# Attention and a squared-ReLU MLP in one hand-ordered kernel: another order for the first head pair and the weights, and other chunks transposed by TensorE

## The chip, the cores and the metric

The kernel runs on one core of a Trainium2 chip. The metric is device time in microseconds (us) of one execution; lower is better. The kernel before took 880.01, 882.34 and 882.65 us in three runs, a median of 882.34 us. One more execution was profiled: it took 878.6 us, and its span from the first to the last instruction is 876.7 us. All rows come from that execution.

## The reference

```python
# q, k, v: (4, 8, 1152, 64) float32; w_in: (512, 2048); w_out: (2048, 512)
q_pool = q.reshape(B, H, S // 2, 2, D).mean(axis=3)             # 576 queries a head
scores = (1 / sqrt(D)) * matmul(q_pool, k.transpose(0, 1, 3, 2))
scores = scores - max(scores, axis=-1, keepdims=True)
attn = exp(scores)
attn = attn / (sum(attn, axis=-1, keepdims=True) + 1e-09)
x = matmul(attn, v)                    # then (batch, query) rows, heads side by side: (2304, 512)
h = x @ w_in
out = maximum(h, 0) ** 2 @ w_out       # (2304, 512)
```

All products are made of two float16 halves of each float32 operand (a high part and what is left of it, after a scaling by powers of two), in three products each.

## The kernel before

**The work.** Four batches of eight heads are taken as 16 head pairs. Each pair is prepared once (`prep`, L346): its k, q and v are loaded (`LK`, `LQ`, `LV` on SP's queue, L365 and L373), neighbouring queries are summed (`QS`, L384), scales are found, the float16 halves are made (`KA`/`KD`, `QA`/`QD`, `VA`/`VD`, L315 to L343), and k and q are transposed by the DMA engines (`KT` L488, `QT` L503) and copied to a second place (`QX`, L509). Then the pair's queries go through in nine chunks of 128 (`chunk`, L540), 144 chunks in all: scores on TensorE (`S`, six matmuls of 128 rows; in one chunk of nine both heads share the rows and there are twelve), row maximum on VectorE (`MX`, L580), exponential on ScalarE (`EX`, L591). The probabilities must then be transposed, and there are two ways:

- By the DMA engines: high half (`HI`, on ScalarE, GpSimd or VectorE), low half (`LO`, L603, on VectorE or GpSimd), one DMA transpose (`TR`, L615).
- By TensorE, for the chunks listed in `TURNB`: three times three transposing matmuls against the identity into a PSUM bank (`TP`, L658), the high half by ScalarE (`TH`, L667), the low half by VectorE (`TL`, L681).

Every ninth chunk (numbers 6, 15, 24 ...) is the shared one and is always transposed by DMA, even where `TURNB` lists it. Per pair, two groups of 54 matmuls multiply the transposed probabilities by v (`PV`, L723).

**The weights.** `weights` (L946) takes each matrix in eight halves of 1 MB: load (`WL`, L967, SP's queue), two ScalarE passes (`W1`, `W2`), and three VectorE passes `W3` (L982), `W5` (L986) and `W4` (L995; `W4` may go to GpSimd instead). There are two staging buffers, so the load of half c waits for the passes of half c - 2. Then TensorE and VectorE find a scale (`WG`, `WM`, `WS1` to `WS3`), and each quarter is split (`WA` on ScalarE, `WD` on VectorE, L343).

**The MLP.** There are nine blocks of 256 tokens (`block`, L746). A block may start when the four pairs of its batch have passed the chunks that it needs (block 0 after chunk 30, block 1 after chunk 35, blocks 2 and 3 after chunks 66 and 71, and so on; the last three after chunks 138 to 143) and when the weights are split. It normalises and splits its x (`RV` to `XD`), then runs eight times 24 matmuls with w_in (`H`, L865), each followed by `HA`, `G1`, `G2`, `G3` on ScalarE, VectorE and GpSimd, and eight times 12 matmuls with w_out (`O`, L914).

**The order.** Every engine runs its instructions in a fixed order, which a planner (`Plan`, L57) writes before the kernel is built. Each step has a list of engines that it may run on with an assumed cost, the steps that it depends on, and a priority:

```python
prio = cfg("nudge", {}).get(len(self.ops), 0.0) + at + off.get(kind, DEF.get(kind, 0.0)) \
       + (off0.get(kind, 0.0) if at < self.early else 0.0)
```

A lower number goes first. `at` is the number of the chunk that the step belongs to; for a pair's preparation it is `need`, the number of the pair's first chunk; for half c of the weights it is `c * WSP + WOF`. `off` is a number per kind of step, `off0` a second one that is added for steps with `at` below 31, `nudge` a number per single step. On each engine the planner looks at the steps that could start within a slack (`slPE`, `slACT`, ...) of the earliest one and takes the one with the lowest priority. SP issues all DMAs, in the planned order: an issue whose wait is not yet fulfilled holds those behind it.

Of the kernel before, what the change touches and what calls it, by code (L numbers as in the profile page):

```python
# [20 lines left out]
def cfg(k, d):  # L21
    return CFG.get(k, d)

# [187 lines left out]
def kernel(  # L211
# [13 lines left out]
    B, H, S, D = q.shape  # L225
# [7 lines left out]
    KD = DM // 128  # L233
# [76 lines left out]
    def raw(*key):  # L310
        return raws[plan.slot[key][1]]
# [21 lines left out]
    def scale_b(t):  # L333
# [3 lines left out]
        )  # L337

    def pmul(out, x, s0, s1=1.0):
        nc.gpsimd.tensor_scalar(out, x, s0, s1, op0=ALU.mult, op1=ALU.mult)  # L340

    def split_lo(o, x, s, h):
        nc.vector.scalar_tensor_tensor(out=o, in0=x, scalar=s, in1=h, op0=ALU.mult, op1=ALU.subtract)  # L343


    def prep(n):  # L346
        pair = preps[n]["pair"]
        b, hp = divmod(pair, NP)
        need = preps[n]["need"]
        slot = preps[n]["slot"]  # L350
        p0 = preps[n]["old"]
        old = [("S", preps[p0]["last"])] if p0 is not None else []
        oldv = [("PV", *preps[p0]["lastg"])] if p0 is not None else []

        def rk():
            return raw("k", n).rearrange("p (h c d) -> p h c d", h=2, c=9)

        def rv():
            return raw("v", n).rearrange("p (h c d) -> p h c d", h=2, c=9)

        def rq():
            return raw("q", n).rearrange("p (c r d) -> p c r d", c=9, r=2)
# [724 lines left out]
    preps, visits, chunks, groups, pairs_, gidx, eds, exs = [], [], [], [], [], {}, {}, {}  # L1087
# [52 lines left out]
    for n in range(len(preps)):  # L1140
        prep(n)
# [52 lines left out]
```

## Time and profile before

| what | value |
|---|---|
| runs shown | 880.01, 882.34, 882.65 us (median 882.34) |
| profiled execution | 878.6 us, span 876.7 us |
| TensorE busy (PE) | 85% of the span |
| VectorE busy (DVE) | 661.3 us, 75% |
| ScalarE busy (ACT) | 601.0 us, 69% |
| GpSimd busy (POOL) | 380.5 us, 43% |
| mean granted TensorE clock | 0.966 of full speed |
| main DMA queue | 130.05 MB, 74.0% of 16 engines over the span |

How to read it: the shares are means over a kernel with three stages, a first one until the MLP's first block, a middle one until the last chunk, and a tail with the MLP alone. Which engine limits differs between them, so the rows further down are taken stage by stage. Busy time of an engine that is not the limit costs nothing.

### The profile page before, as it was taken

What the parts mean: (1) busy time and instruction counts of PE and PEld (TensorE: products, weight loads), DVE (VectorE), ACT (ScalarE), POOL (GpSimd) and SP (SyncE); (2) the same over time, 40 slices, a digit from 0 to 9 for tenths busy, and PEclk for the clock granted to TensorE, in tenths of its full rate; (3) what the DMA queues carried; (4) which work ended last, traced back from release to release, by engine and by line L of the source; (5) the groups of instructions that cost most, each with busy time, mean ns of one, the idle gap of its engine ahead of it and who ended that gap; (6) DMA issues with size and microseconds to landing.
All of it is one profiled execution on the core that took longest, in us unless ns stands there. A gap on an engine that the chain in (4) does not pass through costs nothing. (4 is left out here: it accounts for less than half of the span.)

```text
span 876.7 us, 15564 instructions
## 1 busy us (share of the span) xinstructions
PE 745.9 (85%) x6077; PEld 501.0 (57%) x6077; DVE 661.3 (75%) x838; ACT 601.0 (69%) x957; POOL 380.5 (43%) x274
## 2 busy tenths in 40 slices
PE   1367766577679998999799999999999899999997
PEld 0234454444457565754576667558665666857673
DVE  5788999999998788878988788897889783422120
ACT  5468669668877779787789768679868873524250
POOL 1155542335368445656686337634854740000000
PEclk9999987899879999999999999999999999999999
DMA  7986776885587989989999998899999975000001
GB/s 256 302 208 99 144 195 173 167 184 100 111 174 138 199 166 211 165 176 166 203 181 178 171 181 171 177 172 180 173 190 192 157 136 94 13 13 13 13 13 25
DMA packets 337545, 131.04 MB, mean 149 GB/s; under 512 B 320832, under 2 KB 320832, under 8 KB 337472
## 3 DMA queue, kind: packets, MB, share of 16 engines
q1 hardware_dynamic: 337472, 130.05, 74.0%
q8 instruction: 48, 0.79, 0.4%
q14 instruction: 25, 0.20, 0.1%
HBM read 45.09 MB, written 4.72 MB: 57 GB/s over the span
## 5 line engine op out<-in xcount | busy, mean ns | idle before, releaser
L580 DVE TENSOR_REDUCE ca<-s 128x1 f32<-128x1152 f32 x144 | 192.6, 1348 | 11.9 <-PE s L572 8.6
L603 POOL TENSOR_TENSOR buf<-buf,buf 128x1152 f16<-128x1152 f32 x65 | 163.8, 2522 | 86.2 <-ACT buf L595 67.7
L591 ACT ACTIVATE buf<-s,ca,esc 128x1152 f32<-128x1152 f32 x144 | 188.8, 1311 | 8.4 <-DMA PT<-buf 0.9
L865 PEld LDWEIGHTS <-w 128*128 128x128 f16 x1728 | 168.7, 99 | 29.5 <-issue 3.6
L572 PE MATMUL s<-kT,qT 128*128 128x512 f16 (+1 forms) x768 | 152.4, 340 | 35.9 <-ACT buf L591 24.4
L914 PE MATMUL ba<-w,region 128*128 128x512 f16 x624 | 142.8, 379 | 0.9 <-DVE region L797 0.4
L914 PEld LDWEIGHTS <-region 128*128 128x128 f16 x864 | 83.2, 98 | 94.1 <-issue 2.1
L865 PE MATMUL ba<-region,w 128*128 128x256 f16 x1104 | 126.4, 273 | 2.0 <-DVE PT L681 1.3
L572 PEld LDWEIGHTS <-qT 128*128 128x128 f16 x768 | 69.0, 102 | 102.5 <-issue 41.0
L723 PE MATMUL ba<-PT,v 128*64 128x256 f16 (+1 forms) x1728 | 119.5, 297 | 6.2 <-DVE PT L681 5.5
L723 PEld LDWEIGHTS <-v 128*64 128x64 f16 x1728 | 102.8, 114 | 22.3 <-issue 14.0
L590 ACT ACTIVATE ca<-ca,cols,esc 128x1 f32<-128x1 f32 x144 | 54.8, 381 | 58.1 <-DVE ca L580 57.6
L603 DVE TENSOR_TENSOR buf<-buf,buf 128x1152 f16<-128x1152 f32 x47 | 79.6, 1694 | 19.7 <-ACT buf L595 13.4
L892 DVE TENSOR_TENSOR region<-region 128x512 f16<-128x512 f32 x39 | 39.3, 1009 | 69.3 <-ACT region L885 69.2
L340 POOL TENSOR_SCALAR buf<-buf,cols 128x1152 f16<-128x1152 f32 x30 | 40.4, 1348 | 74.1 <-ACT buf L591 51.8
L658 PE MATMUL ba<-ident,buf 128*128 128x128 f32 x288 | 52.3, 303 | 21.6 <-DVE PT L681 16.6
L595 ACT ACTIVATE buf<-buf 128x1152 f16<-128x1152 f32 x58 | 67.4, 1162 | 3.2 <-DMA PT<-buf 1.1
L667 ACT ACTIVATE PT<-ba 128x384 f16<-128x384 f32 x96 | 44.5, 483 | 32.6 <-PE ba L658 27.8
L892 POOL TENSOR_TENSOR region<-region 128x512 f16<-128x512 f32 x33 | 48.1, 1460 | 31.8 <-ACT region L885 24.5
L658 PEld LDWEIGHTS ba<-ident,buf 128*128 128x128 f32 x288 | 33.9, 152 | 40.4 <-DVE PT L681 25.2
L343 DVE SCALAR_TENSOR_TENSOR buf<-raw,psc,buf 128x576 f16<-128x576 f32 x48 | 53.3, 1147 | 4.6 <-POOL buf L317 3.8
L681 DVE TENSOR_TENSOR PT<-ba,PT 128x384 f16<-128x384 f32 x96 | 50.7, 549 | 4.8 <-ACT PT L667 4.4
(133 smaller groups left out, 949.5 us busy)
## 6 DMA issues: line engine op xcount, KB each, us to landing
raw<-in_k_dram SPq DMA_DIRECT2D x16, 576.0 KB, 4.8
raw<-in_q_dram SPq DMA_DIRECT2D x32, 288.0 KB, 4.4
raw<-in_v_dram SPq DMA_DIRECT2D x16, 576.0 KB, 4.4
region<-in_moe_w_in_dram SPq DMA_DIRECT2D x8, 1024.0 KB, 6.1
region<-in_moe_w_out_dram SPq DMA_DIRECT2D x8, 1024.0 KB, 6.1
out_dram<-buf SPq DMA_DIRECT2D x36, 128.0 KB, 2.4
PT<-buf SPq DMA_TRANSPOSE x128, 4.8
qT<-buf SPq DMA_TRANSPOSE x32, 4.2
```

Of the source, the lines that this page charges most:

```text
L343: nc.vector.scalar_tensor_tensor(out=o, in0=x, scalar=s, in1=h, op0=ALU.mult, op1=ALU.subtract)
L572: nc.tensor.matmul(s[:, x, :w], lhsT=qt[:, l, h, c0 : c0 + 2, :].rearrange("p a b -> p (a b)"), rhs=rhs, **st)
L580: nc.vector.reduce_max(a[:, 0:1], st3(), axis=AX.X)
L590: nc.scalar.activation(a[:, 1:2], a[:, 0:1], AF.Identity, bias=ln14, scale=tl["esc", n][:, 0:1])
L591: nc.scalar.activation(P(), st3(), AF.Exp, bias=a[:, 1:2], scale=tl["esc", n][:, 2:3], accum_out=col)
L595: nc.scalar.activation(hl()[:, 0], P(), AF.Copy)
L603: e.tensor_tensor(out=hl()[:, 1], in0=P(), in1=hl()[:, 0], op=ALU.subtract)
L658: nc.tensor.matmul(t[:, y], lhsT=P()[:, c * 128 : (c + 1) * 128], rhs=ident, is_transpose=True, start=(y == 0), stop=False, skip_group_che ...
L723: nc.tensor.matmul(px[h * 64 : (h + 1) * 64, :N], lhsT=vv[:, h, kc, vl, :], rhs=t[:, 9 * pl + kc, :N], start=(i == 0), stop=(i == 3 * NC - ...
L865: nc.tensor.matmul(ph[:, f2], lhsT=w16[0][:, SLOT[f // 4], wl, a, f % 4 * 128 : (f % 4 + 1) * 128], rhs=xhl()[:, xl, a], start=(i == 0), s ...
L892: e.tensor_tensor(out=gt[u][:, 1], in0=rt[u % 2], in1=gt[u][:, 0], op=ALU.subtract)
L914: nc.tensor.matmul(p[:, :DM], lhsT=g[:, gl, f % 2, tt * 128 : (tt + 1) * 128], rhs=w16[1][:, SLOT[f // 4], wl, f % 4], start=(f == 0 and g ...
```

## The change

The code changes in one line of `prep`, and the table of constants `CFG` is replaced as a whole. The diff, with the long line broken up and cut to what is used below:

```diff
-CFG = {'SPLIT': 0, 'TURN': [],
-  'TURNB': [0, 1, 3, 4, 6, 7, 9, 10, 12, 13, 15, 16, 18, 19, 21, 22, 24, 25, 27, 28, 30, 31, 33, 34,
-            40, 49, 58, 67, 76, 85, 94, 103, 112, 121, 130, 139],
-  'WSP': 0.1, 'WOF': 21.58, 'MSP': 113.61, 'pen': 1179.24, 'bl': 2.88,
-  'slPE': 18.29, 'slACT': 71.85, 'slDVE': 10.76, 'slPOOL': 168.16, 'slSP': 469.69,
...
-  'nudge': {0: 4.83, 1: -37.14, 2: 6.88,
...
+CFG = {'SPLIT': 0, 'TURN': [],
+  'TURNB': [0, 2, 4, 6, 8, 10, 12, 14, 16, 18, 20, 22, 24, 26, 28, 30, 32, 34,
+            38, 44, 50, 56, 62, 68, 74, 80, 86, 92, 98, 104, 110, 116, 122, 128, 134],
+  'WSP': 1.668, 'WOF': 0.15, 'MSP': 16.28, 'pen': 805.54, 'bl': 2.27,
+  'slPE': 253.17, 'slACT': 48.62, 'slDVE': 147.59, 'slPOOL': 732.63, 'slSP': 123.78,
...
@@ prep
-        need = preps[n]["need"]
+        need = preps[n]["need"] if n else cfg("P0", -1000)
```

- `P0` is not set, so every step of the first pair's preparation gets 1000 taken off its priority number.
- `TURNB`: leaving out the shared chunks, TensorE turns 20 of the first 36 chunks before and 16 after, and 12 of the later 108 before and 17 after; in all 32 before and 33 after.
- The 1662 single `nudge` numbers are gone, and nearly all numbers of `off` and `off0` are others.

Sums of `off` and `off0` for steps with `at` below 31, to which `at` is still added:

| step | before | after |
|---|---|---|
| `WL` (weight load) | -156 | 640 |
| `LK`, `LQ`, `LV` (loads of a pair) | 702, -456, 32 | -77, -318, -927 |
| `KT`, `QT` (transposes of a pair) | 123, 814 | -70, -133 |
| `TR` (transpose of a chunk by DMA) | 2583 | 80 |
| `W3`, `W5`, `W4` | 935, 2196, 62 | 0, 0, 480 |
| `MX`, `TL` | 341, -2344 | 0, 0 |
| `WS1`, `WD` | 3414, 257 | -287, -100 |
| `S` | 2168 | 723 |

For later steps `off` alone counts: `S` 2350 before and 728 after, `H` 3380 and 998, `O` 3483 and 1003, `RV` 382 and 968, `XD` 520 and 875, `MX` 735 and 0. The weights' `at` is 21.6 to 23.1 before and 0.15 to 25.2 after.

## Rows read from the trace of the kernel before

**Rows 1.** The page, busy time and share of the span: TensorE.

```profile
PE 745.9 (85%) x6077; PEld 501.0 (57%) x6077; DVE 661.3 (75%) x838; ACT 601.0 (69%) x957; POOL 380.5 (43%) x274
```

**Rows 2.** Busy time by stretch: start:end, length, engines, granted clock, DMA share, GB/s.

```profile
core 0: us, PE busy (x) PEld busy (x) DVE busy (x) ACT busy (x) POOL busy (x), PEclk, DMA share, GB/s
0.00:249.00 249.00, 147.92 (x1208) 101.24 (x1208) 221.72 (x312) 173.99 (x266) 95.29 (x72) 0.90 0.75 178
...
300.00:400.00 100.00, 92.15 (x785) 60.44 (x784) 83.02 (x104) 78.18 (x127) 52.49 (x35) 1.00 0.93 177
...
600.00:700.00 100.00, 96.45 (x811) 67.44 (x810) 84.02 (x95) 81.66 (x132) 62.55 (x44) 1.00 1.01 181
...
745.00:877.00 132.00, 126.65 (x901) 83.86 (x898) 30.48 (x50) 45.47 (x71) 2.59 (x7) 0.99 0.06 15
...
249.00:720.00 471.00, 446.32 (x3750) 300.32 (x3749) 400.01 (x461) 372.60 (x607) 278.15 (x191) 0.99 0.94 175
```

**Rows 3.** Two lines' instructions: duration min/median/max in ns, first and last start in us.

```profile
L865 PE MATMUL ba<-buf,w x192: 270/273/418, 249.4 to 282.9; 128*128 128x256 f16 x192
...
L572 PE MATMUL s<-kT,qT x768: 217/379/635, 43.4 to 719.6; 128*128 128x512 f16 x128, 128*128 128x128 f16 x64
```

**Rows 4.** Two stretches within the first stage, columns as in Rows 2.

```profile
0.00:50.00 50.00, 10.87 (x75) 8.25 (x75) 33.32 (x54) 24.82 (x26) 9.37 (x16) 1.00 0.85 264
60.00:98.00 38.00, 28.45 (x229) 17.57 (x229) 34.46 (x47) 30.55 (x58) 21.23 (x15) 0.96 0.56 94
```

**Rows 5.** Groups of instructions from 60 to 98 us: busy us, mean ns.

```profile
L580 DVE TENSOR_REDUCE ca<-s 128x1 f32<-128x1152 f32 x12 | 16.2, 1348 | 2.1 <-PE s L567 2.1
```

**Rows 6.** Timeline of the start: start us, duration us, engine, line, idle before.

```profile
6.04 1.12 ACT L973 ACTIVATE w<-region 128x1024 f32<-128x1024 f32 x1 [4.03 <-DMA region<-in_moe_w_in_dram]
...
11.38 1.16 ACT L424 ACTIVATE buf<-raw 128x1152 bf16<-128x1152 f32 x1 [0.60 <-DMA raw<-in_k_dram]
...
21.05 3.67 SPq L488 DMA_TRANSPOSE kT<-buf  x1
...
37.08 2.62 SPq L503 DMA_TRANSPOSE qT<-buf  x2
```

**Rows 7.** Groups of instructions from 0 to 249 us: busy us, mean ns.

```profile
L580 DVE TENSOR_REDUCE ca<-s 128x1 f32<-128x1152 f32 x41 | 55.2, 1348 | 4.6 <-PE s L572 2.5 <-PE s L567 2.1
L681 DVE TENSOR_TENSOR PT<-ba,PT 128x384 f16<-128x384 f32 x63 | 32.8, 549 | 1.9 <-ACT PT L667 1.7
...
L343 DVE SCALAR_TENSOR_TENSOR w<-w,wS 128x2048 f16<-128x2048 f32 x6 | 14.9, 2482 | 0.9 <-ACT w L315 0.8
L986 DVE SCALAR_TENSOR_TENSOR w<-region,w 128x1024 int32<-128x1024 int32 x12 | 14.5, 1219 | 0.2
L995 DVE TENSOR_TENSOR w<-w,region 128x1024 f32<-128x1024 f32 x9 | 13.9, 1547 | 0.6
...
L603 DVE TENSOR_TENSOR buf<-buf,buf 128x1152 f16<-128x1152 f32 x7 | 11.2, 1598 | 0.5 <-ACT buf L595 0.4
...
L995 POOL TENSOR_TENSOR w<-w,region 128x1024 f32<-128x1024 f32 x3 | 9.1, 3045 | 15.0 <-DVE w L986 15.0
...
L982 DVE TENSOR_SCALAR w<-w 128x1024 int32<-128x1024 int32 x12 | 8.5, 712 | 5.4 <-ACT w L973 5.4
```

**Rows 8.** The chain that ended last, in order of time: start us, duration us, what.

```profile
586.21 0.48 PE ba L658 x3
...
798.97 10.48 PE bt L865 x96
809.45 10.36 PE bt L914 x48
```

**Rows 9.** One line's instructions on VectorE: duration min/median/max in ns, first and last start.

```profile
L343 DVE SCALAR_TENSOR_TENSOR buf<-raw,psc,buf x48: 798/812/2924, 18.7 to 676.5; 128x576 f16<-128x576 f32 x48
```

**Rows 10.** The page, DMA issues: KB each where given, us to landing.

```profile
PT<-buf SPq DMA_TRANSPOSE x128, 4.8
```

More of the change, by code (lines that the diff above doesn't have):

```diff
@@ new lines @@
+CFG = {'SPLIT': 0, 'TURN': [], 'TURNB': [0, 2, 4, 6, 8, 10, 12, 14, 16, 18, 20, 22, 24, 26, 28, 30, 32, 34, 38, 44, 50, 56, 62, 68, 74, 80, 86, 92, 98, 104, 110, 116, 122, 128, 134], 'WSP': 1.668, 'WOF': 0.15, 'MSP': 16.28, 'pen': 805.54, 'bl': 2.27, 'slPE': 253.17, 'slACT': 48.62, 'slDVE': 147.59, 'slPOOL': 732.63, 'slSP': 123.78, 'off': {'ED': 3.52, 'EX': 0.0, 'G1': 7.57, 'G2': -327.77, 'G3': -712.51, 'GE': 106.11, 'GF': 11.28, 'GM': 7.35, 'GR': -83.1, 'GS': -1554.06, 'GT': -483.92, 'GU': -943.96, 'GW': -608.85, 'H': 998.13, 'HA': 10.05, 'HI': 377.45, 'KA': 232.61, 'KD': 45.75, 'KT': -37.51, 'LK': 178.06, 'LO': 0.72, 'LQ': -446.41, 'LV': -890.99, 'MX': -0.36, 'O': 1002.78, 'OD': -136.82, 'PV': 5.84, 'QA': 1161.12, 'QD': 2.42, 'QK': -788.49, 'QQ': -490.45, 'QS': -624.29, 'QT': -130.75, 'QV': 44.07, 'QX': -736.0, 'RB': 697.5, 'RT': 179.66, 'RU': -42.77, 'RV': 967.54, 'S': 728.2, 'ST': 651.1, 'TH': -2.8, 'TL': -0.45, 'TP': 223.84, 'TR': 26.67, 'VA': 719.74, 'VD': -0.52, 'W1': -5.34, 'W2': 7.86, 'W3': 0.0, 'W4': 36.64, 'W5': 1.5, 'WA': -59.96, 'WD': 181.92, 'WG': 6.6, 'WL': 180.89, 'WM': -115.09, 'WS1': -308.61, 'WS2': -41.81, 'WS3': 18.25, 'XA': 738.07, 'XD': 874.54, 'XM': 838.79, 'XN': 168.03, 'XQ': -6.7, 'XR': -25.78, 'XT': 0.0, 'XU': 94.88, 'XW': 10.01}, 'off0': {'ED': 19.7, 'EX': 1.01, 'G1': 44.88, 'G2': -74.75, 'G3': 109.76, 'GE': -8.18, 'GF': -61.9, 'GM': -3.34, 'GR': -9.85, 'GS': 8.14, 'GT': 63.75, 'GU': 6.06, 'GW': -288.87, 'H': 34.55, 'HA': -8.75, 'KA': 15.81, 'KD': -539.25, 'KT': -32.95, 'LK': -254.97, 'LO': 205.23, 'LQ': 128.8, 'LV': -36.39, 'MX': 0.34, 'O': 22.13, 'OD': 319.51, 'PV': 195.02, 'QA': 22.78, 'QD': 1.87, 'QK': -403.17, 'QQ': 91.93, 'QS': -23.54, 'QT': -2.01, 'QV': 3.19, 'QX': 8.95, 'RB': -51.42, 'RT': 17.45, 'RU': -96.74, 'RV': 17.25, 'S': -5.7, 'ST': 299.89, 'TH': 5.76, 'TP': -260.82, 'TR': 53.57, 'VA': -160.55, 'VD': -209.53, 'W1': 7.54, 'W2': -5.28, 'W3': -0.41, 'W4': 443.7, 'W5': -1.5, 'WA': 37.68, 'WD': -281.84, 'WG': -47.46, 'WL': 458.79, 'WM': -80.6, 'WS1': 21.36, 'WS2': -123.29, 'WS3': -260.63, 'XA': -110.52, 'XD': 12.63, 'XM': 11.88, 'XN': -21.54, 'XQ': -51.95, 'XT': -93.0, 'XU': 70.78, 'XW': -103.32}}
```

1 line of the change is left out of this document (removed).

## The prediction

> **What bounds the kernel now.** I read the totals first, then the stages, then the start, then the pieces on VectorE and the chain. By the totals TensorE is busy for 745.9 us of 876.7 [rows 1], so its idle time is 131 us, and the stages show where it lies [rows 2]. From 0 to 249 us it idles for 101 us while VectorE is busy for 221.7 of 249. From 249 to 720 us it idles for 24.7 us in 471, and in the tail for about 5. The cut at 249 us is no accident: the first `H` matmul starts at 249.4 us, and the last scores at 719.6 us [rows 3]. Until the MLP's first block may start, TensorE has only the chunks, whose pace VectorE sets; from then on it has MLP work to fill every gap. So the kernel is bound by VectorE up to the first `H` and by TensorE after it, and the end moves with two things: when the first `H` starts, and how many chunks are already done by then.
>
> **A formula for the end.** From the first `H` to the end are 627.7 us, of which some 30 are idle (24.7 and 5.3) [rows 2]. A block costs 2 x 10.48 us for `H` (96 of its 192 matmuls take 10.48) and 2 x 10.36 for `O` [rows 8], nine blocks 375 us. The other 222 us belong to the chunks left: 41 row maxima were taken by 249 us [rows 7], so 103 were left, at 2.16 us of TensorE each. Hence
>
> end = T + 375 + 2.16 x (144 - n) + 30,
>
> with T the start of the first `H` and n the chunks done by then: 249 + 375 + 222 + 30 = 876.
>
> T itself: the first scores start at 43.4 us [rows 3]. With almost no weight work, from 60 to 98 us, 12 chunks pass in 38 us [rows 4, 5], 3.17 us each. So 43.4 + 41 x 3.17 = 173.4, and the other 75.6 us up to 249 are weight work after the first scores and losses. A chunk done ahead of the first `H` costs 3.17 us and saves 2.16 later, so each one fewer there gains 1.0 us.
>
> **First pair ahead.** In the kernel before two weight loads stand ahead of the first pair's k, whose first use is at 11.4 us; the pair's own arithmetic is ready for `KT` at 21.1 us, but `QT` is issued at 37.1 us, behind weight loads that wait for their buffers, and the first scores follow 6.3 us later [rows 3, 6]. A first load is used at 6.0 us [rows 6], so k can be taken about 5 us earlier, `QT` be issued at 16 us, and the first scores start at about 22 us (an estimate from these rows). The bounds are 22 and 43: if `QT` still stood behind a weight load, nothing would be won. I take 22, since in the changed list every step of this pair is 1000 ahead of all others on every queue, SP's among them. But this gain is not all kept. VectorE is busy for 33.3 us of the first 50 [rows 4], with weight passes for the most part. By the first scores it had done six halves, 0.71 + 1.22 + 1.22 us each with the short `W4` [rows 7], 19 us. What isn't done then must be done later; while the new order waits for pair 0, it may do two halves (6 us). So 13 us of weight work move behind the first scores, and the start is worth 21 - 13 = 8 us.
>
> **Weights among the chunks.** After the change `W3` and `W5` of half c stand at 1.67c + 0.15 beside `MX` at i, so the weights are spread evenly over chunks 0 to 25 and `WD` follows at once, while block 0 needs chunk 30. Before, 41 chunks were done when the weights were; I take n = 36 (bounds 33, two chunks after chunk 30, and 47, below), a gain of 5 us.
>
> **`W4` to GpSimd.** Its number goes from 62, ahead of `MX`, to 480, behind it, and the planner gives GpSimd a step where VectorE has more urgent work waiting. Before, ten of sixteen ran on VectorE, 13.9 us for nine [rows 7]. The bounds are 0 and 15 us off T; I take 5, since GpSimd takes 3.05 us for one [rows 7] and the choice is unclear. Here a row speaks against the change: the split of k on VectorE takes 812 ns in the median, but up to 2924 [rows 9], so something holds VectorE back by up to 2.1 us at a time, and the nearest suspect is GpSimd at work beside it. The Trainium skill, SBUF — State Buffer, section "SBUF: two separate sides", says that GpSimd and a VectorE instruction with two SBUF inputs share a pair of ports under an exclusive lock, and that whoever comes second is blocked for the whole instruction. By that rule a step moved to GpSimd isn't free, the 5 us would go and the sum would be 5 us higher; the trace agrees in so far as the longest split exceeds the median by not much less than one GpSimd instruction. The median split shows that most steps aren't held, so I keep the 5 us and make the hold a rival.
>
> **Fewer turned early, more later.** Four chunks fewer turned among the first 36 take 4 x 3 x 549 ns = 6.6 us from VectorE [rows 7] and add four `LO`, of which VectorE took a good third (7 of 19 early, 1.6 us each) and some `HI`: net about 3 us off T. TensorE's own part, 4 x 3 x 0.48 us = 5.8 us [rows 8], is hidden, since it idles there. Later it isn't: five chunks more are turned where TensorE is full, 5 x 3 x 0.48 = 7.2 us on the end. Against that stand five DMA transposes fewer, 4.8 us each from issue to landing [rows 10], where the DMA engines are 94% busy [rows 2]; I count that as nothing, since the chain there is TensorE's, not DMA's.
>
> **The other numbers.** The middle stage gets an order without the single-step corrections. Its TensorE idle time lies between 3.5 and 7.9 us in 100 us in the two stretches shown [rows 2], so over 471 us between 17 and 37 us against 24.7 now: -8 to +12. I take +4, since `RV` and `XD` now stand far behind `MX` and a block may be normalised later. In the tail nothing but MLP matmuls is left, and they stay.
>
> **Sum.** 876.7 - 8 (start) - 5 (n) - 5 (`W4`) - 3 (fewer turned) + 7 (more turned) + 4 (middle) = 866.7, or 10 us less. The profiled execution took 878.6 us, so 868.6; the median of the three runs is 882.3, 0.4% above that execution, which would give 872.3. I forecast 869 us.
>
> **Rivals.**
>
> 1. The weights come late, and the kernel is slower. `WL` falls from first (-156) to last (640) on SP's queue, behind every `TR` (80) and every pair load. Place: the loads of halves 4 to 15. While chunks pass at full pace the DMA engines are 56% busy [rows 4], which leaves 44%; a half of 1 MB takes 4 us at the 264 GB/s of the first 50 us [rows 4]; twelve halves need 48 us, which at 44% are 109 us or 34 chunks, nearly the 36 of the forecast. A transpose that waits ahead of a load in the queue tips it over. Price: 1.0 us a chunk beyond 36, so it decides from n = 47 on; at n = 58 the end comes 12 us later than now, 891 us. For it: SP's order and the narrow margin. Against it: chunks slow down while weights are worked on, which leaves the DMA more room.
> 2. Work is moved and not removed: all that VectorE doesn't do at the start it does later, and the `W4` stay where they are. Then the 8 and the 5 us fall away, n and fewer turned chunks (8 us) stand against more turned ones (7 us), and the end is at 869 + 13 = 882 us, the median of now. For it: VectorE is already busy for 89% of the first stage [rows 2].
> 3. GpSimd stands in VectorE's way: seven steps more on GpSimd (five `W4`, two `LO`), each holding VectorE back by the 2.1 us above [rows 9], put 15 us on T in place of 8 off it: 869 + 8 + 15 = 892 us. Against it: GpSimd is busy for only 95 us of 249 [rows 2], and the median split is short. (The rule of the Trainium skill, SBUF — State Buffer, named above, speaks for this rival.)
> 4. More than forecast: all `W4` leave VectorE (10 us more), n is 33 (3 more), and the middle stage reaches its best stretch (12 more): 844 us.
>
> **Numbers.** Forecast 0.50, rival 1 0.20, rival 2 0.14 (mostly no change), rival 3 0.08, rival 4 0.08. A measurement of this kernel tells about 0.3% (2.6 us) from no change. Faster: forecast and rival 4, 0.58; same: 0.11, out of rival 2; slower: rivals 1 and 3 and the rest of 2, 0.31. The forecast's own range, by the bounds of `W4`, n and the middle stage, is 852 to 880. The range reaches to most of rival 1 and half of rival 4: 848 to 891.
>
> **What would show it.** Right: the first scores at about 22 us; the first `H` near T = 249 - 8 - 5 x 3.17 - 5 - 3 = 217 us with about 36 row maxima done; ten or more `W4` on GpSimd; TensorE idle for about 30 us in the middle; the last scores near 710 us (103 chunks in 470 us before, 4.6 us each, now 108 from 217 us on). Wrong: first scores still after 35 us (the pair isn't ahead); a first `H` after 250 us with more than 47 chunks done and weight loads spread beyond 150 us (rival 1); k splits far above 1 us in the mean (rival 3); or TensorE idle for more than 40 us after the first `H`, by which the new list of numbers, not one of its steps, would have decided.

## The result, and the profile after

The changed kernel takes 885.88 us (median of 20 runs, 880.99 to 890.46) against 880.22 us for the kernel before (20 runs, 878.4 to 883.7): a ratio of 1.0058, 95% interval 1.0045 to 1.0072. It is 0.6% slower; the forecast was 869 us, 1.3% below 880.22. The profiled execution took 886.4 us, with a span of 884.2 (before: 878.6 and 876.7).

The page after, busy time of the engines, to be read against [rows 1]:

```profile
PE 753.6 (85%) x6086; PEld 500.6 (57%) x6086; DVE 658.8 (75%) x842; ACT 594.0 (67%) x950; POOL 380.5 (43%) x281
```

Hardly anything moves in the totals, so the stages have to be read. Busy time after, by stretch, cut at the first `H` and at the last scores (columns as in [rows 2]):

```profile
0.00:262.50 262.50, 161.03 (x1272) 104.61 (x1273) 227.73 (x309) 186.65 (x279) 139.99 (x94) 0.82 0.82 187
262.50:730.50 468.00, 443.66 (x3747) 299.10 (x3746) 392.22 (x471) 351.15 (x584) 237.16 (x177) 0.99 0.87 165
730.50:884.20 153.70, 148.85 (x1071) 96.94 (x1069) 38.85 (x66) 56.24 (x89) 3.34 (x10) 1.00 0.14 27
```

The first `H` and the first and last scores after (first and last start at the end of the counts), to be read against [rows 3]:

```profile
L865 PE MATMUL ba<-buf,w x192: 269/273/283, 262.5 to 300.2; 128*128 128x256 f16 x192
...
L572 PE MATMUL s<-kT,qT x768: 217/379/634, 24.9 to 730.5; 128*128 128x512 f16 x128, 128*128 128x128 f16 x64
```

The first scores come at 24.9 us in place of 43.4, nearly as forecast (22). But the first `H` comes at 262.5 us in place of 249.4; forecast was 217. After it TensorE idles for 24.3 us up to the last scores and for 4.9 after them, the 30 us of before. VectorE's groups from 0 to 262.5 us (busy us, mean ns), to be read against [rows 7], and then, of GpSimd's, the one of `LO` and the two of `W4`:

```profile
L580 DVE TENSOR_REDUCE ca<-s 128x1 f32<-128x1152 f32 x47 | 62.8, 1347 | 4.8 <-PE s L572 4.7
L681 DVE TENSOR_TENSOR PT<-ba,PT 128x384 f16<-128x384 f32 x54 | 28.8, 549 | 7.0 <-ACT PT L667 6.9
L343 DVE SCALAR_TENSOR_TENSOR buf<-raw,psc,buf 128x576 f16<-128x576 f32 x18 | 25.1, 1424 | 1.6 <-POOL buf L317 1.4 <-ACT buf L315 0.2
L986 DVE SCALAR_TENSOR_TENSOR w<-region,w 128x1024 int32<-128x1024 int32 x12 | 16.5, 1372 | 0.1
...
L982 DVE TENSOR_SCALAR w<-w 128x1024 int32<-128x1024 int32 x12 | 11.7, 974 | 0.3 <-ACT w L973 0.2
L603 DVE TENSOR_TENSOR buf<-buf,buf 128x1152 f16<-128x1152 f32 x4 | 7.0, 1758 | 0.8 <-ACT buf L595 0.6 <-POOL buf L340 0.2
L995 DVE TENSOR_TENSOR w<-w,region 128x1024 f32<-128x1024 f32 x5 | 7.0, 1390 | 0.2
...
L603 POOL TENSOR_TENSOR buf<-buf,buf 128x1152 f16<-128x1152 f32 x23 | 60.9, 2648 | 24.1 <-DVE buf L599 10.6 <-ACT buf L595 10.4 <-issue 2.3
...
L995 POOL TENSOR_TENSOR w<-w,region 128x1024 f32<-128x1024 f32 x7 | 16.9, 2426 | 20.9 <-DVE w L986 18.6 <-DVE psc L440 2.3
...
L995 POOL TENSOR_TENSOR region<-region 128x1024 f32<-128x1024 f32 x3 | 6.9, 2304 | 0.0
```

The same in the kernel before, from 0 to 249 us, of GpSimd's `LO` and of the split of k and q on VectorE (L343):

```profile
L603 POOL TENSOR_TENSOR buf<-buf,buf 128x1152 f16<-128x1152 f32 x12 | 31.5, 2622 | 17.0 <-ACT buf L595 14.0 <-issue 1.5 <-DVE buf L599 1.0
...
L343 DVE SCALAR_TENSOR_TENSOR buf<-raw,psc,buf 128x576 f16<-128x576 f32 x18 | 16.0, 919 | 3.2 <-POOL buf L317 2.5 <-ACT buf L315 0.6
```

47 row maxima are taken before the first `H`, 41 before [rows 7]. The change did take work off VectorE: `TL` 28.8 us for 32.8, `LO` 7.0 for 11.2, `W4` 7.0 for 13.9 in the group shown. But other instructions got longer with nothing changed about them: the 12 `W3` shown here from 8.5 to 11.7 us, the 12 `W5` from 14.5 to 16.5, and the split of k and q from a mean of 0.92 us to 1.42, with a median of 0.82. (It goes the other way too: VectorE's eight copies `QX` take 3.6 us in place of 9.9.) GpSimd has more to do beside them: in this stage it is busy for 140.0 us in place of 95.3, with 23 `LO` in place of 12 and ten `W4` in place of six. VectorE's busy time in this stage is 6.0 us more than before, and its idle time 34.8 us in place of 27.3; at the start it waits for 9.9 us at one stretch, until the first pair's scales can be found, where its longest wait was 5.4.

**The balance.** T is 13.1 us later. From there on 97 chunks are left in place of 103, 6 x 2.16 = 13.0 us less, against 7.2 us for five more turned ones: 13.1 - 13.0 + 7.2 = 7.3 us, and the span is 7.5 longer. So the prediction's formula holds (262.5 + 375 + 2.16 x 97 + 7 + 29 = 883); what it was fed with, T and n, did not.

### The profile page after: what moved, and what is told of

Same layout as the page of the kernel before. It is cut to its first block, busy times and chain, and to the rows that moved or that the text cites. A ratio compares the mean times of both kernels' runs of the same rounds, so it can differ in the third digit from the quotient of the medians.

```text
span 884.2 us, 15570 instructions
## 1 busy us (share of the span) xinstructions
PE 753.6 (85%) x6086; PEld 500.6 (57%) x6086; DVE 658.8 (75%) x842; ACT 594.0 (67%) x950; POOL 380.5 (43%) x281
## 5 line engine op out<-in xcount | busy, mean ns | idle before, releaser
L572 PE MATMUL s<-kT,qT 128*128 128x512 f16 (+1 forms) x768 | 161.2, 354 | 27.4 <-ACT buf L591 23.6
L603 POOL TENSOR_TENSOR buf<-buf,buf 128x1152 f16<-128x1152 f32 x52 | 133.5, 2568 | 75.2 <-ACT buf L595 44.6
L723 PE MATMUL ba<-PT,v 128*64 128x256 f16 (+1 forms) x1728 | 114.4, 289 | 5.7 <-DVE PT L681 2.6
L723 PEld LDWEIGHTS <-v 128*64 128x64 f16 x1728 | 95.4, 111 | 25.4 <-issue 12.8
L603 DVE TENSOR_TENSOR buf<-buf,buf 128x1152 f16<-128x1152 f32 x59 | 93.8, 1591 | 12.9 <-ACT buf L595 8.1
L340 POOL TENSOR_SCALAR buf<-buf,cols 128x1152 f16<-128x1152 f32 x35 | 48.8, 1394 | 75.0 <-ACT buf L591 65.3
L892 DVE TENSOR_TENSOR region<-region 128x512 f16<-128x512 f32 x34 | 28.5, 839 | 64.0 <-ACT region L885 63.9
L892 POOL TENSOR_TENSOR region<-region 128x512 f16<-128x512 f32 x38 | 57.4, 1512 | 32.0 <-ACT region L885 25.7
L343 DVE SCALAR_TENSOR_TENSOR buf<-raw,psc,buf 128x576 f16<-128x576 f32 x48 | 67.0, 1432 | 2.9 <-POOL buf L317 1.4
L667 ACT ACTIVATE PT<-ba 128x384 f16<-128x384 f32 x99 | 46.6, 485 | 33.2 <-PE ba L658 33.0
L595 ACT ACTIVATE buf<-buf 128x1152 f16<-128x1152 f32 x49 | 56.9, 1162 | 1.8
```

The lines of the kernel that those rows point to most:

```text
L572: nc.tensor.matmul(s[:, x, :w], lhsT=qt[:, l, h, c0 : c0 + 2, :].rearrange("p a b -> p (a b)"), rhs=rhs, **st)
L595: nc.scalar.activation(hl()[:, 0], P(), AF.Copy)
L603: e.tensor_tensor(out=hl()[:, 1], in0=P(), in1=hl()[:, 0], op=ALU.subtract)
L723: nc.tensor.matmul(px[h * 64 : (h + 1) * 64, :N], lhsT=vv[:, h, kc, vl, :], rhs=t[:, 9 * pl + kc, :N], start=(i == 0), stop=(i == 3 * NC - ...
L892: e.tensor_tensor(out=gt[u][:, 1], in0=rt[u % 2], in1=gt[u][:, 0], op=ALU.subtract)
```

## What holds VectorE

Two stretches of the timeline after show where the length of a split comes from (start us, duration us). VectorE, from 184.9 us on:

```profile
184.94 0.54 DVE L681 TENSOR_TENSOR PT<-ba,PT 128x384 f16<-128x384 f32 x1
185.40 5.06 DVE L343 SCALAR_TENSOR_TENSOR buf<-raw,psc,buf 128x576 f16<-128x576 f32 x2
190.39 0.55 DVE L681 TENSOR_TENSOR PT<-ba,PT 128x384 f16<-128x384 f32 x1
```

GpSimd in the same time:

```profile
184.03 3.22 POOL L603 TENSOR_TENSOR buf<-buf,buf 128x1152 f16<-128x1152 f32 x1
...
187.20 2.65 POOL L995 TENSOR_TENSOR region<-region 128x1024 f32<-128x1024 f32 x1
```

Two splits that take 0.82 us each in the median took 5.06 us together: they began while GpSimd's `LO` ran (to 187.25), and ended 0.6 us after its `W4` did (189.85).

The whole first stage can be read so, from the start and the duration of each instruction in the two traces. Take each VectorE instruction that lasted over 0.1 us longer than the shortest one of its operation and shape: in every one of them a GpSimd instruction ended, and from that end it went on for the shortest one's duration, less 0.1 to 0.2 us. What they lost is 32.7 us in all (before: 22.8). Of this 18.9 us were lost behind `LO` (before: 8.6) and 6.4 behind `W4` (6.7). So the holds grew by some 10 us, and it was `LO` that grew them, not `W4`. The sentence ahead of the rows that busy time of an engine that is not the limit costs nothing doesn't hold for GpSimd here.

Not every kind of VectorE instruction is held. Durations (min/median/max ns) after, of the maxima, of `TL` and of `W3`, one line of the kernel each:

```profile
L580 DVE TENSOR_REDUCE ca<-s x144: 1330/1348/1359, 27.4 to 730.8; 128x1 f32<-128x1152 f32 x144
...
L681 DVE TENSOR_TENSOR PT<-ba,PT x99: 531/548/558, 33.2 to 695.5; 128x384 f16<-128x384 f32 x99
...
L982 DVE TENSOR_SCALAR w<-w x12: 678/688/2761, 16.1 to 172.3; 128x1024 int32<-128x1024 int32 x12
```

And the groups of instructions after, with different shapes kept apart (busy us, mean ns), of the small scale step at L451:

```profile
L451 DVE TENSOR_SCALAR psc<-psc 128x2 f32<-128x2 f32 x16 | 6.3, 392 | 0.2
...
L451 DVE TENSOR_SCALAR psc<-psc 128x1 f32<-128x1 f32 x16 | 2.4, 149 | 0.2
```

None of the 144 maxima and none of the 99 `TL`, which read PSUM, was ever longer than its median by more than 2%. `W3`, which works in SBUF alone, reached four times its median, and even a step on two numbers a partition has 392 ns in the mean where the one on one number has 149. The Trainium skill, SBUF — State Buffer, section "SBUF: two separate sides", says that a GpSimd instruction and a VectorE instruction that runs in a two-port mode, or that has two SBUF inputs while the GpSimd one reads SBUF, exclude each other, and that the second "fully blocks". The trace agrees for the splits, `W3`, `W5` and `LO`, and in that what reads PSUM isn't touched.

The other thing is the order. What VectorE did between the last `WD` and the first `H` after, 29 us (of its list, block 0's steps at L797, L823, L834 and the last one at L343, and the long ones between them):

```profile
230.98 2.45 DVE L343 SCALAR_TENSOR_TENSOR w<-region,wS,w 128x2048 f16<-128x2048 f32 x1
233.36 0.68 DVE L797 TENSOR_TENSOR x<-x,ba 128x512 f32<-128x512 f32 x1
...
235.22 2.13 DVE L343 SCALAR_TENSOR_TENSOR buf<-raw,psc,buf 128x576 f16<-128x576 f32 x1
...
241.20 0.67 DVE L797 TENSOR_TENSOR x<-x,ba 128x512 f32<-128x512 f32 x1
241.80 3.65 DVE L343 SCALAR_TENSOR_TENSOR buf<-raw,psc,buf 128x576 f16<-128x576 f32 x2
...
247.43 0.43 DVE L823 TENSOR_SCALAR_CACHE_REDUCE ba<-ba 128x256 f32<-128x256 f32 x1
...
251.37 0.15 DVE L834 RECIPROCAL xs<-xs 128x1 f32<-128x1 f32 x1
...
253.70 3.69 DVE L343 SCALAR_TENSOR_TENSOR v<-raw,psc,v 128x576 f16<-128x576 f32 x2
...
259.62 1.27 DVE L343 SCALAR_TENSOR_TENSOR buf<-x,xs,buf 128x1024 f16<-128x1024 f32 x1
```

The weights are split at 233.4 us (before: 244.6), with 40 maxima done, as many as before. But block 0's normalisation stands behind row maxima, the splits of pair 5 and the start of block 1, and is done at 260.9: the first `H` follows the weights by 29 us, where it followed by 4.8 before, and seven more maxima fall into this time.

## The experiments

Theories: VectorE sets T, by its list and by GpSimd's holds; rival 1, late weight loads; rival 2, work moved and not removed; and, for what follows T, whether the five more turned chunks and the list as a whole cost what the prediction said.

**e1: the ten GpSimd `W4` on VectorE.**

```diff
         for o in seq:
+            if o["name"][0] == "W4":
+                o["eng"] = "DVE"
```

> The changed kernel with its ten GpSimd W4 put on VectorE, everything else in the same order. If a step given to GpSimd leaves VectorE free of it (the forecast's pricing), ten W4 at 1.23 us come back to VectorE ahead of the first H: first H near 273 us, end near 896 us. If GpSimd holds VectorE while it works (rival 3), the ten GpSimd instructions of 2.4 us each cost VectorE about as much as they spare it: first H within 4 us of 262.5, end 882 to 889 us, and the mean of the W3 and W5 on VectorE falls from 0.92 and 1.42 us towards their medians of 0.69 and 1.22.

886.14 us, ratio to the kernel before 1.0070 (1.0049 to 1.0092): no difference from the change as it is. The first `H`:

```profile
L865 PE MATMUL ba<-buf,w x192: 269/273/282, 264.6 to 302.4; 128*128 128x256 f16 x192
```

Ten instructions more on VectorE cost 2.1 us of T, not 12. (The change itself had moved four of them: six ran on GpSimd before.) One expectation missed: `W3` and `W5` got no shorter (1.03 and 1.55 us in the mean); the gain lay in the splits of k and q (1.42 to 1.15 us in the first stage). What held the others was not `W4`: behind `LO` VectorE lost 21.8 us here. The Trainium skill, Perfetto Trace Analysis, section "Optimizing Scalar/DVE Operations", warns that moving work between these two engines "might not help"; here the two medians are 0.3 us apart.

**e2: the same ten left out.**

```diff
         for o in seq:
+            if o["name"][0] == "W4" and o["eng"] == "POOL":
+                continue
             o["emit"](o)
```

> The changed kernel without the ten W4 that run on GpSimd (their part of the weights' sign is not put in). Work on GpSimd that VectorE does not feel: first H and end as in the changed kernel, within 2 us (262.5 and 886). GpSimd holding VectorE: ten instructions of 2.4 us gone from beside it, of which VectorE felt 0.6 to 1.5 us each, so the first H comes 6 to 15 us earlier and the end goes to 872 to 880 us.

880.08 us, ratio 1.0008 (0.9990 to 1.0026), so 6 us less than the change; first `H` at 258.5:

```profile
L865 PE MATMUL ba<-buf,w x192: 269/273/282, 258.5 to 296.2; 128*128 128x256 f16 x192
```

GpSimd's work is not free for VectorE: 4.0 us of T for ten instructions, 0.4 us each, where 0.6 to 1.5 were expected; the time is at the edge of the 872 to 880 us expected.

**e3: two weight loads of sixteen.**

```diff
         for o in seq:
+            if o["name"][0] == "WL" and o["name"][1] > 1:
+                continue
             o["emit"](o)
```

> The changed kernel with the first two of its sixteen weight loads alone; the other halves are computed from what lies in the two staging buffers. Rival 1 (late loads set the first H): the first H falls below 240 us and the end to 870 us or less. VectorE's queue sets it: the passes of a half start sooner, but VectorE has as much to do and in the same order, so the first H stays within 6 us of 262.5 and the end between 880 and 888 us.

886.02 us, ratio 1.0070 (1.0047 to 1.0093). First `H`:

```profile
L865 PE MATMUL ba<-buf,w x192: 269/273/283, 258.2 to 296.0; 128*128 128x256 f16 x192
```

With 14 MB fewer to load the first `H` comes 4 us earlier in the profiled execution (882.04 us, the fastest of six), and the median time is the same. Rival 1 falls, though two of its three signs had come true (first `H` after 250 us, and loads issued up to 177.5 us); the third missed by one chunk. A load waits for the passes of the half two before it, so the loads can't run ahead of the passes.

**e4: block 0's normalisation first.**

```diff
+FIRST = ("RV", "RT", "RU", "RB", "XR", "XQ", "XN", "XM", "XT", "XU", "XW", "XA", "XD")
...
-        prio = cfg("nudge", {}).get(len(self.ops), 0.0) + at + ...
+        first = kind in FIRST and len(name) > 1 and name[1] == 0
+        prio = (-900.0 if first else 0.0) + at + ...
```

> The changed kernel with 900 taken off the numbers of block 0's normalisation alone (RV to XD), so that it stands ahead of the row maxima on VectorE. First H near 240 us with about 39 chunks done, in either theory. Formula of the prediction: 240 + 375 + 2.16 x 105 + 7 + 30 = 879 us, so 7 us faster than the changed kernel. Rival: the idle time of TensorE after the first H is no constant but depends on how the whole list of numbers fits; with one group moved the planner writes another order for all that follows, the idle time grows from 29 to about 60 us, and the end comes at 905 to 915 us.

926.05 us, ratio 1.0521 (1.0492 to 1.0549). By stretch, cut at its first `H` and last scores:

```profile
0.00:233.50 233.50, 140.21 (x1070) 90.23 (x1071) 204.17 (x276) 162.04 (x239) 129.97 (x83) 0.81 0.81 190
233.50:755.10 521.60, 469.93 (x3901) 314.28 (x3899) 420.07 (x518) 382.80 (x628) 214.11 (x162) 0.97 0.84 156
755.10:920.80 165.70, 158.24 (x1118) 102.44 (x1116) 39.61 (x66) 58.88 (x92) 9.21 (x12) 0.98 0.14 28
```

T is 233.5 us with 39 maxima done, as expected, and the kernel is 40 us slower all the same. Idle time after T is 51.7 + 7.5 = 59 us in place of 29, as the rival had it, though the time is beyond the rival's 905 to 915 us too: TensorE's work after T takes 628 us where the formula has 375 + 2.16 x 105 + 7 = 609. The granted clock is 0.97 in the middle, not 0.99, in a stage in which TensorE stood idle for twice as long; how much of the 19 us that is isn't shown. Moving one group in the planner's numbers didn't move T alone: the planner wrote another list for all that follows.

**e5: five later chunks not turned** (and not transposed by the DMA engines either).

```diff
         for o in seq:
+            if o["name"][0] in ("TP", "TH", "TL") and o["name"][1] in (50, 68, 86, 104, 122):
+                continue
             o["emit"](o)
```

> The changed kernel with the turning of five later chunks (50, 68, 86, 104, 122) left out: no TP, TH and TL for them, so their columns of the transposed probabilities are old ones. By the forecast's term of +7 for five chunks more turned, TensorE being full after the first H, the end comes 5 x 3 x 0.48 = 7 us earlier, at 879 us. Rival: TensorE waits somewhere in each 100 us anyway, and what it doesn't turn becomes idle time: end within 2 us of 886, and the idle time after the first H grows from 24 us to about 30.

879.43 us, ratio 0.9989 (0.9975 to 1.0003), 6.5 us less than the change. The middle stage:

```profile
262.30:723.60 461.30, 435.94 (x3701) 293.80 (x3700) 383.81 (x455) 345.06 (x569) 239.56 (x177) 0.99 0.88 167
```

TensorE's busy time falls by 7.7 us and its idle time stays (25.4). The prediction's +7 is right to half a microsecond, and without these matmuls the change would tie with the kernel before.

**e6: the kernel before without its single corrections** (`'nudge': {}`).

> The kernel before with its 1662 single corrections taken out and nothing else. The prediction gave losing them -8 to +12 us of idle time in the middle stage, taken as +4. If the corrections carry the order, the end is 6 to 12 us later than before, 884 to 890 us, with TensorE idle for more than 30 us between the first H and the last scores. If not, the end is within 2 us of 879.

889.01 us, ratio 1.0086 (1.0060 to 1.0113): they carry 9 us there. TensorE's idle time between the first `H` (247.4) and the last scores is 29.4 us, 4.7 more than with them, and just not the more than 30 expected.

**e7 and e8: both kernels in another order.** Same steps on the same engines. Places in the lists were exchanged as long as a replay of the lists, with durations from the two traces, got shorter. Both kernels get the same edit:

```diff
+ORDER = [...]
+SLOTS = "..."
...
     seq = plan.order(("EX", NSTEP - 1))
+    seq, deal = [plan.ops[i] for i in ORDER], iter(SLOTS.split())
+    for o in seq:
+        if o["take"]:
+            x = next(deal)
+            plan.slot[o["take"][0]] = ({"b": "buf", "r": "raw", "a": "a", "t": "t"}[x[0]], int(x[1]))
```

> The changed kernel, same steps on the same engines, with the order rearranged step by step wherever a step stood waiting on its engine ahead of another that could go (in all stages; the steps were timed with the durations of the two traces). If the changed kernel's loss lies in its order: first H at about 246 us with still 47 chunks done, TensorE idle for less than 20 us after it, end 246 + 375 + 2.16 x 97 + 7 + 15, about 853 us, 860 with some loss. If the loss lies in what the change gives to whom (GpSimd holding VectorE, more turned chunks), it stays above 880 us.

> The kernel before with its order rearranged in the same manner, same steps on the same engines. If order is what counts: first H at about 238 us with 42 chunks done, end 238 + 375 + 2.16 x 102 + 15, about 848 us, 858 with some loss; so as good as the changed kernel rearranged, or better by the changed kernel's 7 us for five more turned chunks. If its own order already fits, it stays within 4 us of 879.

882.66 us (ratio 1.0025, 1.0008 to 1.0042) and 883.12 us (1.0027, 1.0007 to 1.0047): neither as fast as expected; the first `H` came at 264.9 and 249.4. In e7 block 8's squares are written before the product of block 7's first 128 tokens has read its own. Up to the first `H`, VectorE's busy time fell by 4.5 us in e7 and 8.1 in e8, and its idle time rose by 6.9 and 8.1: what the lists saved there came back as waits. That the replay had the holds wrong is the likely reason, and isn't shown.

**e9 and e10: the same with the holds in the replay.** Each VectorE instruction that works in SBUF waits there for the GpSimd instruction under way, and the other way round. The edit is that of e7, with other lists.

> The changed kernel, same steps on the same engines, rearranged once more. The first rearrangement took no account of which VectorE instructions GpSimd holds (the splits, LO, HI, W3 to W5 and copies that read and write SBUF alone; never the maxima, which read PSUM); this one sets those beside GpSimd's idle time. If holds and waits are what the first stage lost: first H at 230 to 245 us with 47 chunks done, the mean k split below 1.1 us (1.43 before the rearrangement), end 240 + 375 + 2.16 x 97 + 7 + 20, about 850 us. If holds can't be ordered away, the first H stays at 262 and the end at 880 or more.

> The kernel before, same steps on the same engines, rearranged in the same manner. If holds and waits are what the first stage lost: first H at 225 to 240 us with 41 chunks done, end 235 + 375 + 2.16 x 103 + 20, about 850 us, so level with the changed kernel rearranged, whose five more turned chunks weigh against its head start. If the choice of work in the change is the better one, the changed kernel rearranged is at least 5 us ahead of this one.

839.81 us, ratio 0.9545 (0.9521 to 0.9569), and 834.98 us, ratio 0.9480 (0.9452 to 0.9508), with the first `H` at 237.5 and 223.3 us and 47 and 42 maxima done. Both times are below the 850 us expected, and e10, with the work of the kernel before, isn't level with e9 but 4.8 us ahead. In e10 block 7's x is written before block 6's seventh `H` has read the old one; e12 has this in sequence. The page of e9:

```profile
PE 740.4 (88%) x6086; PEld 495.8 (59%) x6086; DVE 601.0 (72%) x842; ACT 588.9 (70%) x950; POOL 367.6 (44%) x281
```

Its stretches, cut at its first `H` and last scores:

```profile
0.00:237.50 237.50, 153.91 (x1273) 101.97 (x1274) 206.45 (x303) 184.70 (x278) 136.61 (x90) 0.86 0.87 203
237.50:682.10 444.60, 437.46 (x3747) 296.86 (x3746) 354.16 (x474) 347.85 (x583) 225.44 (x180) 1.00 0.92 173
```

Its `W5` (min/median/max ns; its lines stand four further down):

```profile
L990 DVE SCALAR_TENSOR_TENSOR w<-region,w x12: 1209/1222/1226, 16.2 to 159.1; 128x1024 int32<-128x1024 int32 x12
```

The same 842 VectorE instructions take 601.0 us in place of 658.8; the longest `W5` of this group is 1.23 us in place of 2.19. In the first stage VectorE's busy time falls by 21.3 us and its idle time by 3.7: these are the 25 us by which the first `H`, again with 47 maxima done, is earlier. After it TensorE idles for 7.1 us up to the last scores in place of 24.3 and takes 6.2 us less for its work, at a granted clock of 1.00 in place of 0.99. So of the 46.6 us by which the span is shorter, some 21 are VectorE instructions that were held less; that the holds caused what was won after the first `H` too isn't shown.

**e11: the first pair ahead, in the kernel before.**

```diff
     seq = plan.order(("EX", NSTEP - 1))
+    for names, after in (
+        ((("QT", 0),), ("KT", 0)),
+        ((("QX", 0),), ("W4", 3)),
+        ((("S", 0), ("S", 1)), ("WG", 0, 1)),
+        ((("MX", 0),), ("W4", 4)),
+        ((("MX", 1),), ("W4", 5)),
+    ):
+        moved = [plan.ops[plan.at[x]] for x in names]
+        seq = [o for o in seq if o not in moved]
+        x = seq.index(plan.ops[plan.at[after]]) + 1
+        seq[x:x] = moved
```

> The kernel before with the first pair's QT, QX, first two scores and their maxima moved ahead of the weight work that stood before them; nothing else moves. First scores at 29 to 31 us in place of 43.4. The forecast priced such a head start of 13 us at 13 x 8/21, 5 us, so the first H would come at 244 and the end at 872 us. Rival 2 (work moved, not removed): VectorE does the same passes in another order, first H between 249 and 253 us, end 878 to 883 us.

883.74 us, ratio 1.0035 (1.0020 to 1.0050). First `H` and first scores:

```profile
L865 PE MATMUL ba<-buf,w x192: 269/273/421, 251.7 to 285.2; 128*128 128x256 f16 x192
...
L572 PE MATMUL s<-kT,qT x768: 217/379/634, 28.5 to 722.7; 128*128 128x512 f16 x128, 128*128 128x128 f16 x64
```

The scores start 15 us earlier and the first `H` 2.3 us later, with the same 41 maxima done. In this kernel rival 2 was right about the start.

**e12: e10 with the sequence of a block's `H` kept.**

> The kernel before rearranged once more from the order of the run before it, now with the H of a block kept in sequence (that order let block 7's x be written before block 6's seventh H had read the old one) and with more exchanges. First H at 218 to 226 us with 41 chunks done, TensorE idle for about 10 us after it: 222 + 375 + 2.16 x 103 + 10, about 829 us. If keeping the sequence costs what the earlier order had won, it ends near 840 us, level with the changed kernel rearranged.

831.93 us, ratio 0.9460 (0.9434 to 0.9485), the fastest of all. Its first two stretches:

```profile
0.00:220.50 220.50, 139.32 (x1205) 93.14 (x1205) 196.61 (x306) 172.06 (x264) 90.45 (x71) 0.94 0.83 197
220.50:669.00 448.50, 436.65 (x3729) 298.23 (x3726) 362.00 (x454) 368.11 (x601) 272.14 (x189) 1.00 0.98 182
```

With the work of the kernel before, the first `H` comes at 220.6 us with 41 maxima done, 29 us earlier than before. The changed kernel rearranged (e9) is 7.9 us behind, about the 6.5 us that e5 gives for its five more turned chunks. But e12's list comes from more exchanges, so which choice of work is better isn't settled to the microsecond. Settled is that the kernel before could be made 5% faster with its own choice of work, by order alone.

## Why the prediction was wrong, point by point

- **The formula**, made from the kernel before, held for the change (883 by it, 884.2 measured), not for e4: the 30 us of idle time are a property of one list, not of the kernel.
- **The step that failed** is T = 217. It took VectorE's work to be the sum of its instructions' durations, each with a price of its own, and the first `H` to follow the weights at once. Of the 16 us that start, `W4` and fewer turned chunks were to give, some 6 came: at 3.17 us a chunk, 249.4 - 41 x 3.17 = 119.4 us are left before and 262.5 - 47 x 3.17 = 113.5 after. And 47 chunks were done in place of 36. With both put in, 217 + 10 + 11 x 3.17 = 262, against 262.5. The end missed by less, 884.2 us of span for 866.7: about 10 us are the gains that didn't come, 11 us the chunks at 1.0 us each, and the middle stage gives 4 back.
- **n, 36:** 47, the larger part of the miss in T. The weights were split 11 us earlier, but with 40 maxima done and not 36, and nothing in the list made block 0 follow: the other seven were taken in the 29 us up to the first `H`. The prediction saw that `RV` and `XD` stand far behind `MX`, and priced that for the later blocks only. That block 0's place in the list set T is borne out by e4: with these steps first, the first `H` comes at 233.5 us with 39 maxima done.
- **Start, -8:** the first scores came 18.5 us earlier. In the kernel before, 15 us of it were worth nothing (e11); in the changed kernel no run tried it alone. Passes done later are done in full.
- **`W4`, -5:** no more than 2 us of T and nothing of the time, near the lower bound given: all ten put back cost 2.1 us of T (e1), and the change had moved four. The hold was named there, and the row that spoke against the change [rows 9] was outvoted because the median split was short. A median can't show this; the mean does: 1.15 us before, 1.43 after for the split of k and q over the whole kernel, as these two lines of the page (before, then after) show. The kernel's own planner reckons with the hold, and the prediction didn't use it: the planner lets VectorE's steps of the kinds in `LOCK`, the splits, `W3` to `W5` and `LO` among them, wait for the GpSimd step under way; `MX` and `TL` aren't in that list.

```profile
L343 DVE SCALAR_TENSOR_TENSOR buf<-raw,psc,buf 128x576 f16<-128x576 f32 x48 | 53.3, 1147 | 4.6 <-POOL buf L317 3.8
```

```profile
L343 DVE SCALAR_TENSOR_TENSOR buf<-raw,psc,buf 128x576 f16<-128x576 f32 x48 | 67.0, 1432 | 2.9 <-POOL buf L317 1.4
```

- **More turned later, +7:** 6.5 (e5). **Middle, +4:** -0.4; the new list has no more idle time without corrections than the old one with them, though in the kernel before they are worth 9 us (e6).
- **Fewer turned early, -3:** `TL` and `LO` gave back 8 us of VectorE's time; no run tried this alone.
- **Rivals:** 1 had the signs and not the cause (e3). 2 was right on the start. 3 was right that GpSimd stands in VectorE's way, but not on the size and not on which step does it: it counted five `W4` and two `LO` more at 2.1 us each, 15 us; there are four `W4` and eleven `LO` more in the first stage, and the holds grew by some 10 us. The end came between rivals 2 and 3.
- **The range:** 885.88 us lies above the forecast's own range, 852 to 880, and inside the last one, 848 to 891. That is luck: the last one reached so far for rival 1, whose cause wasn't at work.

## What to carry to other kernels

Before pricing a step at its duration, compare the mean of its group with its shortest. Where they differ, look which engine's instruction ends inside the long ones: a step moved to that engine may win little, and what else runs there counts as well. Ask of every early finish what the next step in the list is: the weights were ready 11 us earlier, and the steps that use them stood 29 us behind. A head start (e11) and one group put first (e4) won nothing here in lists of hundreds of fixed places; lists fitted to the durations on the chip won 5%, more than either choice of who does what.

## What was not expected of the hardware

- The holds take at least 58 us of VectorE's 659 over the kernel, as e9 shows by the same instructions in another order.
- A step on two numbers a partition is held (392 ns in the mean, up to 2.3 us) where the same step on one number isn't (149).
- Fourteen loads of 1 MB fewer, in a stage with the DMA engines busy for 82% of the time, changed the median time by 0.1 us (e3).
